# Spreading the late parts of 1/den through a copy inside DRAM, in a fused linear-attention and top-8 MLP kernel

## The chip, the cores and the metric

The kernel runs on one core of a Trainium2 chip. TensorE (PE) multiplies matrices, VectorE (DVE), ScalarE (ACT) and GpSimd (POOL) work on vectors, SyncE (SP) issues transfers. ScalarE and GpSimd can issue transfers too; what an engine issues goes out in the order of its own instructions, and an instruction that waits holds all behind it. All transfers run on the core's 16 DMA engines. The metric is the device time of one execution in microseconds (us), lower is better.

## The reference

One sequence of S = 2048 rows of D = 640. With 32 heads of 20 columns each:

```python
xn = layernorm(x)                                  # no gain, no bias
q, k, v = split(xn @ wqkv)                         # 32 heads of 20
pq, pk = phi(q), phi(k)                            # phi(t) = t + 1 if t > 0 else exp(t)
kv = einsum("hsd,hse->hde", pk, v);  z = pk.sum(s)
o = (pq @ kv) / (pq . z + 1e-6)                    # den: one number per row and head
A = o @ wo
idx = the 8 rows with the largest r = xn @ w_r
y = ((silu(xn[idx] @ w_gate) * (xn[idx] @ w_up)) @ w_down) * sigmoid(r[idx])
out = x + A + xn + scatter(y at idx)
```

Inputs and output are bf16.

## The kernel before

The rows are 16 tiles of 128 (`T`), the columns 5 chunks of 128 (`KC`). Instructions are issued in the order in which the program lists them; nothing reorders them within an engine.

The first 55 us or so load x, normalise it, and form k and part of q. The products over k are gathered into `G`, then into one matrix `Ms` that holds kv and wo together (`m_unit`, five units), so that the last stage is one product: tile t of the output is `pqT` (phi(q), transposed: columns of q on the partitions, rows of the sequence along the free axis) times `Ms`, plus x and xn. That stage is the loop `for t in range(T - 1)` with `o_mm(t)` (two halves of 320 columns, 10 matmuls) on TensorE and `o_out(t)` on VectorE, which adds `x_sb[:, t, :]` (by then x + xn) and hands the tile to a transfer. Its output buffer is one of four per parity of t, so tile t + 8 reuses that of tile t.

Before `o_mm(t)` the columns of `pqT` of that tile must be divided by den, which has one number per head and row while `pqT` has 20 partitions per head. The kernel spreads 1/den over the partitions through DRAM. `den_mm` forms den in PSUM, with the heads on 32 partitions and four groups of rows beside each other; `den_act` makes 1/den by Ln and Exp. For rows 0 to 1023 this is done once (`rden_out`, `rden_in`, ScalarE's queue out and SP's back). Rows 1024 to 1535 are the third quarter, `rden2`; rows 1536 to 2047 the fourth, `rden3`. Each of these leaves in four parts of 128 rows by `rden_out_b`: a part reads a 32 x 128 block and writes each of its rows 20 times into `rdb`, 640 rows of 256 bytes. `rden_in_b` brings 640 x 512 numbers back into `spare`, and `rden_mul_b(t)` on VectorE multiplies tile t of `pqT` by them, two tiles ahead of its use: after `o_out(6)` comes the multiply for tile 8, after `o_out(10)` that for tile 12.

The eight chosen rows go through the small MLP meanwhile: `gate_up`, then `down` (48 small matmuls after `o_mm(0)`), and ScalarE's four steps into `y8`. Tiles 11 to 15 of x + xn lie in DRAM as well (`s_dram`, written by `load_s`); GpSimd adds `y8` there, and `x_sb[:, 11:16]` is read back from it, so tiles from 11 on wait for that reload. For the tiles before, GpSimd adds `y8` to the output in DRAM, after `o_out(10)`.

[...]

The four parts of `rden2` are on SP, those of `rden3` on ScalarE and SP by turns. ScalarE issues the outputs of tiles 0 to 3 and the odd ones, and the reload of `x_sb`; SP those of 4, 6, ..., 14.

Of the kernel before, what the change touches and what calls it, by code (L numbers as in the profile page):

```python
# [8 lines left out]
P = 128  # L9
S = 2048  # L10
D = 640
H = 32
DH = D // H
F = 1536
T = S // P
KC = D // P
FC = F // P
# [9 lines left out]
TS = 11  # L27
NS = TS * P

BF16 = mybir.dt.bfloat16  # L30
# [8 lines left out]
def kernel(  # L39
# [12 lines left out]
    nc = tc.nc  # L52
    V, A, G, PE = nc.vector, nc.scalar, nc.gpsimd, nc.tensor
# [12 lines left out]
    def sb(name, shape, dtype=BF16):  # L66
        return sm.tile(shape, dtype, tag=name, name=name)

    ps = psum.tile([P, 8, 512], F32, tag="ps", name="ps")
    rd = tc.dram_tile([4, D, 256], BF16, name="rd")  # L70
    rdb = [tc.dram_tile([D, 512], BF16, name=f"rd{tb}") for tb in (2, 3)]
    s_dram = tc.dram_tile([S - NS, D], BF16, name="s_dram")

    x_sb = big.tile([P, T, D], BF16, tag="x_sb", name="x_sb")
# [9 lines left out]
    wu = big.tile([P, KC, F], BF16, tag="wu", name="wu")  # L84
# [3 lines left out]
    SP = nc.sync  # L88
# [20 lines left out]
    def kcw(w, src, lo, hi):  # L109
        SP.dma_start(w[:, lo:hi, :], src.rearrange("(kc p) n -> p kc n", p=P)[:, lo:hi, :])  # L110
# [7 lines left out]
    def load_wo():  # L118
        half = NB // 2
        for i in range(2):  # L120
            src = bass.AP(
                tensor=A_wo.tensor, offset=A_wo.offset + i * (D // 2) * D,
                ap=[[D, EB], [3 * DH * D, half], [1, D]],
            )
            SP.dma_start(wo[0:EB, i * half : (i + 1) * half, :], src)
# [4 lines left out]
    def load_wd(lo, hi):  # L130
        SP.dma_start(wd[:, lo:hi, :], B_w_down.rearrange("(fc p) n -> p fc n", p=P)[:, lo:hi, :])
# [139 lines left out]
    def q_mm(u, bank=7):  # L271
        tb, m = u // KC, u % KC
        for kc in range(KC):
            PE.matmul(  # L274
                ps[:, bank, :], lhsT=wq[:, kc, m * P : (m + 1) * P],
                rhs=xnT[:, kc, tb * 512 : (tb + 1) * 512],
                start=(kc == 0), stop=(kc == KC - 1),
            )

    def q_act(u, bank=7):  # L280
        e = evq.tile([P, 512], BF16, tag="eq", name=f"eq{u}")
        r = evq.tile([P, 512], BF16, tag="rq", name=f"rq{u}")
        A.activation(e[:], ps[:, bank, :], AF.Exp)  # L283
        A.activation(r[:], ps[:, bank, :], AF.Relu)  # L284
        kev["q", u] = e, r

    def q_phi(u):
        tb, m = u // KC, u % KC
        e, r = kev.pop(("q", u))
        V.scalar_tensor_tensor(  # L290
            out=pqT[:, m, tb * 512 : (tb + 1) * 512], in0=e[:], scalar=1.0, in1=r[:],
            op0=ALU.min, op1=ALU.add,
        )

    def q_ev(u, bank=7):
        q_act(u, bank)
        q_phi(u)
# [208 lines left out]

    load_cols(wv, 0, KC, 2 * D)
    load_wo()
    kcw(wu, B_w_up, 2, 3)
    kcw(wu, B_w_up, 3, KC)  # L510
    for i in range(0, FC, 4):
        load_wd(i, i + 4)
    PE.transpose(psb[0:T, 1, 0:P], r_all[:], ident[:])
    g1(T - 4)
    r_row = sb("r_row", [T, P], F32)
# [49 lines left out]
    def den_mm(o, w, bank):  # L565
        for kc in range(KC):
            for j in range(4):
                PE.matmul(
                    ps[32 * j : 32 * j + 32, bank, 0:w], lhsT=zm[:, kc, :],
                    rhs=pqT[:, kc, o + j * w : o + (j + 1) * w],  # L570
                    start=(kc == 0), stop=(kc == KC - 1), tile_position=(0, 32 * j),
                )

    def den_act(o, w, bank):
        ld = sm.tile([P, w], F32, tag="ld", name=f"ld{o}")
        rden = sb(f"rden{o}", [P, w])
        A.activation(ld[:], ps[:, bank, 0:w], AF.Ln, bias=cst["eps6"][:])
        A.activation(rden[:], ld[:], AF.Exp, scale=-1.0)
        return rden
# [11 lines left out]
            rd[j : j + 2, :, :].rearrange("j (m p) t -> p (j m) t", p=P),  # L591
        )

    def rden_out_b(eng, i, rden, j):
        eng.dma_start(  # L595
            rdb[i][:, j * P : (j + 1) * P].rearrange("(h i) t -> h i t", i=DH),
            rden[32 * j : 32 * j + 32, :].unsqueeze(1).to_broadcast([32, DH, P]),
        )

    def rden_in_b(i):  # L600
        SP.dma_start(sprb[i], rdb[i][:, :].rearrange("(m p) t -> p m t", p=P))

    def rden_mul(j):
        sl = pqT[:, :, j * 256 : (j + 1) * 256]
        V.tensor_tensor(out=sl, in0=sl, in1=spr[:, j * KC : (j + 1) * KC, :], op=ALU.mult)

    def rden_mul_b(t):
        sl = pqT[:, :, t * P : (t + 1) * P]
        V.tensor_tensor(  # L609
            out=sl, in0=sl, in1=sprb[t // 12][:, :, t % 4 * P : (t % 4 + 1) * P], op=ALU.mult  # L610
        )
# [18 lines left out]
    def m_unit(m, b0, eng):  # L630
        for h in range(2):
            for i in range(2):
                b = 2 * m + i
                PE.matmul(  # L634
                    ps[HB * i : HB * (i + 1), b0 + h, 0:HW], lhsT=kvz[0:EB, b * HB : (b + 1) * HB],
                    rhs=wo[0:EB, b, h * HW : (h + 1) * HW], start=True, stop=True,
                    tile_position=(0, HB * i),
                )
        dst = Ms[:, m, :].rearrange("p (b f) -> p b f", b=2)
        eng(dst, ps[:, b0 : b0 + 2, 0:HW])  # L640
# [80 lines left out]
                        start=(kc == 0), stop=(kc == KC - 1), tile_position=(0, 32 * j),  # L721
                    )

    def down():
        for fc in range(FC):
            for i in range(4):
                PE.matmul(
                    ps[32 * i : 32 * i + 32, 5 + 2 * (i % 2), 0:QW], lhsT=hT[:, 32 * fc : 32 * fc + 32],
                    rhs=wd[:, fc, i * QW : (i + 1) * QW],
                    start=(fc == 0), stop=(fc == FC - 1), tile_position=(0, 32 * i),  # L730
                    skip_group_check=True,
                )
# [29 lines left out]
    for u, b in ((13, 4), (14, 5), (15, 0), (16, 3)):  # L762
        q_mm(u, b)
        q_ev(u, b)
    m_unit(4, 6, V.tensor_copy)
    den_mm(1024, P, 4)
    rden2 = den_act(1024, P, 4)
    for j in range(4):
        rden_out_b(SP, 0, rden2, j)
    for u, b in ((17, 5), (18, 2), (19, 4)):  # L770
        q_mm(u, b)
        q_act(u, b)
        if u < 19:
            rden_mul(u - 17)
        q_phi(u)
    rden_in_b(0)

    def o_mm(t):
        b0 = 2 * (t % 2)
        for b in range(2):  # L780
            for kc in range(KC):
                PE.matmul(  # L782
                    ps[:, b0 + b, 0:HW], lhsT=pqT[:, kc, t * P : (t + 1) * P],
                    rhs=Ms[:, kc, b * HW : (b + 1) * HW],
                    start=(kc == 0), stop=(kc == KC - 1),
                )

    def o_out(t):
        b0 = 2 * (t % 2)
        o_t = evk.tile([P, 2, HW], BF16, tag=("ek", "rk")[t % 2], name=f"o{t}")  # L790
        V.tensor_tensor(  # L791
            out=o_t[:], in0=ps[:, b0 : b0 + 2, 0:HW],
            in1=x_sb[:, t, :].rearrange("p (b f) -> p b f", b=2), op=ALU.add,
        )
        eng = nc.sync if t % 2 == 0 and t > 2 else nc.scalar
        eng.dma_start(out_v[:, t, :], o_t[:].rearrange("p b f -> p (b f)"))

    def o_last(t):
# [24 lines left out]
    for t in range(T - 1):  # L823
        o_mm(t)
        if t == 0:
            down()
            den_mm(1536, P, 6)
            rden3 = den_act(1536, P, 6)
            for j in range(4):
                rden_out_b((A, SP)[j % 2], 1, rden3, j)  # L830
            rden_in_b(1)
            for i in range(4):
                A.activation(  # L833
                    y8[:, i * QW : (i + 1) * QW], ps[32 * i : 32 * i + C, 5 + 2 * (i % 2), 0:QW],
                    AF.Identity, scale=gate[32 * i : 32 * i + C, 2:3],
                )
            G.indirect_dma_start(  # L837
                s_dram[:, :], bass.IndirectOffsetOnAxis(ap=idx_i[0:C, 1:2], axis=0), y8[:], None,
                bounds_check=S - NS - 1, oob_is_err=False, compute_op=ALU.add,
            )  # L840
        if t == 5:
            A.dma_start(x_sb[:, TS:T, :], s_dram[:, :].rearrange("(t p) d -> p t d", p=P))
        o_out(t)
        if t < 2:
            rden_mul(t + 2)
        if 6 <= t < 14:
            rden_mul_b(t + 2)
        if t == TS - 1:
            G.indirect_dma_start(
                out[0, 0:NS, :], bass.IndirectOffsetOnAxis(ap=idx_i[0:C, 0:1], axis=0), y8[:], None,  # L850
                bounds_check=NS - 1, oob_is_err=False, compute_op=ALU.add,
            )
# [29 lines left out]
```

## Time and profile before

| | |
|---|---|
| timed runs, us | 113.39, 114.22, 117.89 (median 114.22) |
| the profiled execution, us | 112.75 |
| its span, from first to last instruction, us | 111.0 |
| granted TensorE clock | 1.00 |
| bytes moved by DMA | 23.65 MB, 213 GB/s in the mean |
| packets under 512 bytes | 14194 of 31655 |

The profile follows one execution, whose own time is 112.75 us; its span leaves out 1.75 us around it. "Busy" counts the time in which an engine had an instruction at work. SPq and ACTq are the transfers' issue instructions on SP and ScalarE. A DMA's "landing" is the time from its issue to its completion, so it holds the time in which it stood behind others. Line numbers (L595) are those of the kernel before.

### The profile page before, as it was taken

What the parts mean: (1) busy time and instruction counts of PE and PEld (TensorE: products, weight loads), DVE (VectorE), ACT (ScalarE), POOL (GpSimd) and SP (SyncE); (2) the same over time, 40 slices, a digit from 0 to 9 for tenths busy, and PEclk for the clock granted to TensorE, in tenths of its full rate; (3) what the DMA queues carried; (4) which work ended last, traced back from release to release, by engine and by line L of the source; (5) the groups of instructions that cost most, each with busy time, mean ns of one, the idle gap of its engine ahead of it and who ended that gap; (6) DMA issues with size and microseconds to landing.
All of it is one profiled execution on the core that took longest, in us unless ns stands there. A gap on an engine that the chain in (4) does not pass through costs nothing.

```text
span 111.0 us, 2501 instructions
## 1 busy us (share of the span) xinstructions
PE 104.3 (94%) x897; PEld 61.8 (56%) x906; DVE 81.2 (73%) x186; ACT 58.9 (53%) x155; POOL 39.2 (35%) x86
## 2 busy tenths in 40 slices
PE   5899999999999999999999999999999999994990
PEld 2256645555555555564447788534457776662660
DVE  1798997789999996544349745696799766884780
ACT  1449996797877666555058352788894400000000
POOL 6903563211344448899993420000000050000040
PEclk9999999999999999999999999999999999999999
DMA  3999435792679998999999949369868199999243
GB/s 81 324 328 297 152 68 101 197 240 59 183 189 203 210 177 206 224 220 302 235 388 365 304 110 287 98 173 302 292 91 151 51 344 254 242 359 386 89 124 118
DMA packets 31655, 23.65 MB, mean 213 GB/s; under 512 B 14194, under 2 KB 30362, under 8 KB 31642
## 3 DMA queue, kind: packets, MB, share of 16 engines
q1 hardware_dynamic: 25168, 18.97, 64.3%
q10 hardware_dynamic: 6410, 4.51, 13.2%
q8 instruction: 7, 0.11, 0.5%
q14 instruction: 6, 0.05, 0.2%
q0 software_dynamic: 64, 0.01, 0.2%
HBM read 15.44 MB, written 6.08 MB: 194 GB/s over the span
## 4 chain that ended last, share of the span: by engine, by line
PE 73%; DMA 14%; ACT 3%; issue 3%; DVE 2%; ACTq 2%; SPq 0%
PE ps L274 19%; PE ps L237 19%; PE ps L266 16%; PE ps L782 5%; DMA spare<-rd 5%; DMA out_dram<-o 4%; PE ps L502 4%; DMA rd<-rden 3%; DMA x_sb<-in_A_x_dram 2%; PE ps L617 2%; PE ps L634 2%; PE ps L717 2%; PE ps L215 1%; PE ps L808 1%; ACTq L595 1%
## 5 line engine op out<-in xcount | busy, mean ns | idle before, releaser
L237 PE MATMUL ps<-wk,xnT 128*128 128x320 bf16 (+1 forms) x160 | 25.0, 300 | 0.1
L274 PE MATMUL ps<-xnT,wq 128*128 128x512 bf16 x93 | 22.9, 379 | 0.6 <-issue 0.3
L782 PE MATMUL ps<-late,pqT 128*128 128x320 bf16 x150 | 21.6, 299 | 1.4 <-DVE pqT L609 1.4
L237 PEld LDWEIGHTS <-xnT 128*128 128x128 bf16 x160 | 15.1, 98 | 8.7 <-ACT xnT L221 0.9
L266 PE MATMUL ps<-pk,xn 128*128 128x512 bf16 x78 | 19.5, 379 | 0.1
L251 ACT ACTIVATE ek<-ps 128x320 bf16<-128x320 f32 x32 | 14.8, 463 | 8.1 <-PE ps L237 8.1
L782 PEld LDWEIGHTS <-pqT 128*128 128x128 bf16 x150 | 14.1, 98 | 8.7 <-DVE pqT L609 3.1
L283 ACT ACTIVATE eq<-ps 128x512 bf16<-128x512 f32 x20 | 11.9, 597 | 9.0 <-PE ps L274 9.0
L175 DVE BATCH_NORM_STATS2 stats<-x_sb 128x6 f32<-128x320 bf16 x32 | 14.8, 474 | 2.3 <-DMA x_sb<-in_A_x_dram 2.3
L290 DVE SCALAR_TENSOR_TENSOR pqT<-eq,rq 128x512 bf16<-128x512 bf16 x20 | 13.7, 685 | 3.7 <-ACT rq L284 3.7
L259 DVE SCALAR_TENSOR_TENSOR pk<-ek,rk 128x640 bf16<-128x640 bf16 x16 | 13.0, 813 | 4.2 <-ACT rk L252 4.2
L791 DVE TENSOR_TENSOR o<-ps,x_sb 128x640 bf16<-128x640 f32 x15 | 12.3, 823 | 4.7 <-PE ps L782 3.5
L274 PEld LDWEIGHTS <-wq 128*128 128x128 bf16 x100 | 9.3, 98 | 10.7 <-issue 0.7
L252 ACT ACTIVATE rk<-ps 128x320 bf16<-128x320 f32 x32 | 14.8, 463 | 0.0
L207 POOL TENSOR_SCALAR x_sb<-x_sb,rs,nm 128x640 bf16<-128x640 bf16 x13 | 13.8, 1068 | 0.6
L266 PEld LDWEIGHTS <-xn 128*128 128x128 bf16 x80 | 7.7, 98 | 8.1
L284 ACT ACTIVATE rq<-ps 128x512 bf16<-128x512 f32 x20 | 11.9, 593 | 0.0
L186 POOL TENSOR_SCALAR t<-mv 128x1 bf16<-128x1 f32 x12 | 3.8, 316 | 21.7 <-DVE mv L177 21.4
L818 ACT CAST o<-ps 128x160 bf16<-128x160 f32 x1 | 0.3, 292 | 19.1 <-PE ps L808 19.1
L187 POOL TENSOR_TENSOR rs<-t,mhalf 128x1 f32<-128x1 bf16 x12 | 10.0, 834 | 1.0
L837 POOL DMA_INDIRECT s_dram<-y,idx_i x1 | 1.6, 1594 | 23.2 <-ACT y L833 23.2
L196 DVE TENSOR_SCALAR xn<-x_sb,mv,rs 128x640 bf16<-128x640 bf16 x16 | 7.2, 450 | 3.3 <-POOL rs L187 2.8
(123 smaller groups left out, 98.6 us busy)
## 6 DMA issues: line engine op xcount, KB each, us to landing
spare<-rd SPq DMA_DIRECT2D x4, 640.0 KB, 5.4
wg<-in_B_w_gate_dram SPq DMA_DIRECT2D x5, 384.0 KB, 3.4
wd<-in_B_w_down_dram SPq DMA_DIRECT2D x3, 640.0 KB, 13.5
out_dram<-o ACTq DMA_DIRECT2D x9, 160.0 KB, 4.0
rd<-rden ACTq DMA_DIRECT2D x1, 1280.0 KB
wu<-in_B_w_up_dram SPq DMA_DIRECT2D x3, 384.0 KB, 3.5
wo<-in_A_wo_dram SPq DMA_DIRECT2D x2, 500.0 KB, 7.7
x_sb<-in_A_x_dram SPq DMA_DIRECT2D x3, 320.0 KB, 5.8
```

The source lines that it names most:

```text
L175: V.bn_stats(out=stats[:, t, b, :], in_=x_sb[:, t, b * HW : (b + 1) * HW])
L207: G.tensor_scalar(out=x_sb[:, t, :], in0=x_sb[:, t, :], scalar1=rs1[:, sl], scalar2=nm[:, sl], op0=ALU.mult, op1=ALU.add,)
L237: PE.matmul(ps[:, b0 + b, 0:n], lhsT=xnT[:, kc, t * P : (t + 1) * P], rhs=wk[:, kc, b * HW : b * HW + n], start=(kc == 0), stop=(kc == KC ...
L251: A.activation(e[:, b, :], ps[:, b0 + b, 0:HW], AF.Exp)
L252: A.activation(r[:, b, :], ps[:, b0 + b, 0:HW], AF.Relu)
L259: V.scalar_tensor_tensor(out=pk[:, t, :].rearrange("p (b f) -> p b f", b=2), in0=e[:], scalar=1.0, in1=r[:], op0=ALU.min, op1=ALU.add,)
L266: PE.matmul(ps[:, 2 + c, :], lhsT=xn[:, t, c * P : (c + 1) * P], rhs=pk[:, t, 0:512], start=(t == 0), stop=(t == T - 1),)
L274: PE.matmul(ps[:, bank, :], lhsT=wq[:, kc, m * P : (m + 1) * P], rhs=xnT[:, kc, tb * 512 : (tb + 1) * 512], start=(kc == 0), stop=(kc == K ...
L283: A.activation(e[:], ps[:, bank, :], AF.Exp)
L290: V.scalar_tensor_tensor(out=pqT[:, m, tb * 512 : (tb + 1) * 512], in0=e[:], scalar=1.0, in1=r[:], op0=ALU.min, op1=ALU.add,)
L782: PE.matmul(ps[:, b0 + b, 0:HW], lhsT=pqT[:, kc, t * P : (t + 1) * P], rhs=Ms[:, kc, b * HW : (b + 1) * HW], start=(kc == 0), stop=(kc == ...
L791: V.tensor_tensor(out=o_t[:], in0=ps[:, b0 : b0 + 2, 0:HW], in1=x_sb[:, t, :].rearrange("p (b f) -> p b f", b=2), op=ALU.add,)
```

## The change

- `rden_out_b` now writes each part of a late quarter once per head, 32 rows of 256 bytes, into a small DRAM tensor `rdh` (32 x 512). A new `rden_copy` reads each of its rows 20 times and writes `rdb` with 640 rows of 1,024 bytes, DRAM to DRAM, on SP.
- The four parts of `rden3` are all on ScalarE; `rden_copy(1)` is on SP, behind `rden_in_b(0)`, and `rden_in_b(1)` comes after tile 0's output.
- `den_mm(1536)` stands in the middle of `down`; `den_mm(1024)` ahead of `m_unit(4)`.
- SP issues the outputs of tiles 0, 2, 3, 6, 8, 9, 10, 12, 14, ScalarE those of 1, 4, 5, 7, 11, 13. The reload of `x_sb` moves from ScalarE to SP, behind the outputs of tiles 2 and 3 there.
- The late loads of `wu` (1 + 2 chunks) become one, those of `wd` two instead of three.

Rows 0 to 1023 of 1/den go as before. The engines' instructions are otherwise the same, in the same order. On SP the order from the third quarter on is: four parts of `rden2`, copy of the third quarter, its reload, copy of the fourth, output of tile 0, the fourth's reload, outputs of tiles 2 and 3, reload of `x_sb`, outputs of 6, 8, 9, 10, 12, 14, first half of 15.

```diff
+    rdh = [tc.dram_tile([H, 512], BF16, name=f"rdh{tb}") for tb in (2, 3)]
...
-    kcw(wu, B_w_up, 2, 3)
-    kcw(wu, B_w_up, 3, KC)
-    for i in range(0, FC, 4):
-        load_wd(i, i + 4)
+    kcw(wu, B_w_up, 2, KC)
+    for i in range(0, FC, 6):
+        load_wd(i, i + 6)
...
-    def rden_out_b(eng, i, rden, j):
-        eng.dma_start(
-            rdb[i][:, j * P : (j + 1) * P].rearrange("(h i) t -> h i t", i=DH),
-            rden[32 * j : 32 * j + 32, :].unsqueeze(1).to_broadcast([32, DH, P]),
+    def rden_out_b(eng, i, rden):
+        for j in range(4):
+            eng.dma_start(rdh[i][:, j * P : (j + 1) * P], rden[32 * j : 32 * j + 32, :])
+
+    def rden_copy(i):
+        SP.dma_start(
+            rdb[i][:, :].rearrange("(h i) t -> h i t", i=DH),
+            rdh[i][:, :].unsqueeze(1).to_broadcast([H, DH, 512]),
         )
...
-    def down():
-        for fc in range(FC):
+    def down(lo, hi):
+        for fc in range(lo, hi):
...
+    den_mm(1024, P, 4)
     m_unit(4, 6, V.tensor_copy)
-    den_mm(1024, P, 4)
     rden2 = den_act(1024, P, 4)
-    for j in range(4):
-        rden_out_b(SP, 0, rden2, j)
+    rden_out_b(SP, 0, rden2)
+    rden_copy(0)
     for u, b in ((17, 5), (18, 2), (19, 4)):
...
-    rden_in_b(0)
...
-        eng = nc.sync if t % 2 == 0 and t > 2 else nc.scalar
+        eng = nc.sync if t in (0, 2, 3, 9) or t % 2 == 0 and t > 4 else nc.scalar
...
         if t == 0:
-            down()
+            down(0, FC // 2)
             den_mm(1536, P, 6)
+            down(FC // 2, FC)
             rden3 = den_act(1536, P, 6)
-            for j in range(4):
-                rden_out_b((A, SP)[j % 2], 1, rden3, j)
-            rden_in_b(1)
+            rden_out_b(A, 1, rden3)
+            rden_in_b(0)
+            rden_copy(1)
...
+        if t == 2:
+            rden_in_b(1)
         if t == 5:
-            A.dma_start(x_sb[:, TS:T, :], s_dram[:, :].rearrange("(t p) d -> p t d", p=P))
+            SP.dma_start(x_sb[:, TS:T, :], s_dram[:, :].rearrange("(t p) d -> p t d", p=P))
```

## The prediction

> **What bounds the kernel now.** I read the page's busy table, then the chain of waits, the waits by engine and queue, the timeline of the last 35 us, and the DMA answers.
>
> ```profile
> span 111.0 us, 2501 instructions
> ...
> PE 104.3 (94%) x897; PEld 61.8 (56%) x906; DVE 81.2 (73%) x186; ACT 58.9 (53%) x155; POOL 39.2 (35%) x86
> ```
>
> TensorE is busy for 104.3 of 111.0 us. A change that leaves its work alone, as this one does, can win only the idle time. The chain shows where the one long gap near the end comes from (start, length, what):
>
> ```profile
> 93.08 3.19 DMA rd<-rden
> ...
> 96.33 5.34 DMA spare<-rd
> ...
> 101.69 0.50 DVE pqT L609
> ```
>
> The last quarter of 1/den is written to DRAM, read back as `spare`, multiplied into `pqT` for tile 12, and only then TensorE goes on. The waits (total, times, longest) give its price and what delayed it:
>
> ```profile
> PE ps L782 <- DVE pqT L609: 1.4, 1, 1.4
> ```
>
> ```profile
> SPq L595 <- DMA rd<-rden: 5.6, 1, 5.6
> ```
>
> SP stood 5.6 us before it could issue its two parts of that quarter (at 92.15 below), held by a part that ScalarE had issued at 86; the change takes this wait away, since no part is on SP any more. The hole itself is 1.43 us (the timeline below has it to two digits), and the ceiling of the gain in this execution is 1.43 of 112.75 us, 1.3%. The timeline rows used for the rest (start, length, engine, line):
>
> ```profile
> 79.50 0.37 ACT L577 ACTIVATE ld<-ps,eps 128x128 f32<-128x128 f32 x1
> ...
> 79.91 0.31 ACT L578 ACTIVATE rden<-ld 128x128 bf16<-128x128 f32 x1
> 80.24 3.16 SPq L595 DMA_DIRECT2D rd<-rden  x4
> ...
> 83.92 1.01 PE L727 MATMUL ps<-wd,late 128*32 128x160 bf16 x48
> ...
> 85.14 15.67 PE L782 MATMUL ps<-late,pqT 128*128 128x320 bf16 x110
> ...
> 85.71 0.31 ACT L578 ACTIVATE rden<-ld 128x128 bf16<-128x128 f32 x1
> 86.05 1.40 ACTq L595 DMA_DIRECT2D rd<-rden  x2
> 86.12 0.37 SPq L601 DMA_DIRECT2D spare<-rd  x1
> ...
> 89.42 1.59 POOL L837 DMA_INDIRECT s_dram<-y,idx_i  x1 [23.25 <-ACT y L833]
> ...
> 92.15 1.48 SPq L595 DMA_DIRECT2D rd<-rden  x2
> ...
> 93.63 0.39 ACTq L842 DMA_DIRECT2D x_sb<-s_dram  x1
> ...
> 94.31 0.48 DVE L609 TENSOR_TENSOR pqT<-pqT,spare 128x640 bf16<-128x640 bf16 x1
> ...
> 95.09 0.82 DVE L791 TENSOR_TENSOR o<-ps,x_sb 128x640 bf16<-128x640 f32 x1 [0.29 <-PE ps L782]
> ...
> 99.39 0.82 DVE L791 TENSOR_TENSOR o<-ps,x_sb 128x640 bf16<-128x640 f32 x1 [0.17 <-issue]
> ...
> 102.10 0.82 DVE L791 TENSOR_TENSOR o<-ps,x_sb 128x640 bf16<-128x640 f32 x1
> ...
> 102.24 4.44 PE L782 MATMUL ps<-late,pqT 128*128 128x320 bf16 x30 [1.43 <-DVE pqT L609]
> ...
> 105.42 1.35 POOL L849 DMA_INDIRECT out_dram<-y,idx_i  x1 [14.40 <-DMA out_dram<-o]
> ```
>
> Without the hole TensorE would end tile 11 at 85.14 + 15.67 = 100.81 and start tile 12 there. Transfers and their time from issue to landing, then half-microsecond stretches of the whole core (last three columns: clock, DMA share, GB/s):
>
> ```profile
> spare<-rd SPq DMA_DIRECT2D x4, 640.0 KB, 5.4
> ...
> rd<-rden SPq DMA_DIRECT2D x6, 160.0 KB, 3.4
> ...
> x_sb<-s_dram ACTq DMA_DIRECT2D x1, 800.0 KB, 5.4
> ...
> out_dram<-o ACTq DMA_DIRECT2D x1, 80.0 KB, 1.6
> ...
> s_dram<-y,idx_i POOLq DMA_INDIRECT x1, 4.1
> ```
>
> ```profile
> 64.00:64.50 0.50, 0.50 (x7) 0.28 (x5) 0.50 (x2) 0.33 (x1) 0.09 (x1) 1.00 0.06 23
> 68.00:68.50 0.50, 0.50 (x17) 0.50 (x14) 0.19 (x1) 0.00 (x0) 0.00 (x0) 1.00 1.06 294
> 80.50:81.00 0.50, 0.50 (x4) 0.24 (x3) 0.50 (x2) 0.49 (x1) 0.00 (x0) 1.00 0.00 0
> 81.50:82.00 0.50, 0.50 (x4) 0.20 (x2) 0.50 (x2) 0.50 (x2) 0.00 (x0) 1.00 0.78 119
> 82.00:82.50 0.50, 0.50 (x4) 0.23 (x3) 0.50 (x2) 0.50 (x2) 0.00 (x0) 1.00 1.00 154
> 85.50:86.00 0.50, 0.50 (x6) 0.35 (x5) 0.44 (x1) 0.47 (x2) 0.00 (x0) 1.00 0.29 54
> ...
> 100.00:100.50 0.50, 0.50 (x5) 0.36 (x4) 0.21 (x1) 0.00 (x0) 0.00 (x0) 1.00 1.09 389
> ```
>
> They price a transfer in three parts. The broadcast issued at 80.24 begins to move at about 81.6 (0.78 of the slice from 81.50): a start of 1.35 us. It stops at about 85.65 (0.29 of the slice from 85.50) and the queue that waits for it goes on at 86.12: a finish of 0.45. Between them the data goes at 389 GB/s in the reload, 294 in the first broadcast (512-byte rows) and 154 in the late ones (256-byte rows). 640 KB then take 1.7, 2.2 and 4.3 us; a tile written out (160 KB) 0.42; 800 KB reloaded 2.1.
>
> **The change, step by step.** *First hop.* 1/den of the third quarter is ready at 79.91 + 0.31 = 80.22, as before: `den_mm` moves ahead of one unit of M, but ScalarE comes to it straight from q's evictions, with no idle time, at 79.50. Four issues replace four. Each costs between 0.37 (a reload's) and 0.79 (3.16 / 4); with 32 rows in place of 640 I take 0.4. The fourth starts at 81.4. It carries 8 KB; its landing lies between the 1.6 of the small write and the 3.4 of the old parts, and I take 1.6, the nearer in size: 83.0.
>
> [...]
>
> *Copy inside DRAM.* No row shows DRAM to DRAM. Its 640 KB in rows of 1,024 bytes should take no less than 1.7 us and, I take it, no more than the 4.3 of the 256-byte rows; as both sides use DRAM I take the middle, 3.0. Issue at 83.0, landing after 1.35 + 3.0 + 0.45 = 4.8, at 87.8.
>
> [...]
>
> *Third quarter's reload* is issued at 87.8 in place of 86.12 and takes 1.35 + 1.7 + 0.45 = 3.5 alone, 5.4 in the median: 91.3 to 93.2. It is first used at 94.31. The 1.7 us lost are hidden, with 1.1 to 3.0 to spare.
>
> *Fourth quarter.* `den_mm` stands after half of `down`, 0.5 us earlier (half of 1.01): 1/den at 85.71 + 0.31 - 0.5 = 85.5. ScalarE issues four parts (1.6 against 1.40 for two), the last at 86.7, landed at 88.3. What is queued behind them on ScalarE is `y8` and the outputs of tiles 1, 4, 5, 7; `y8` feeds the scatter, which so stays at about 89.4 and lands 4.1 later, 93.5. The copy is queued on SP behind the third quarter's reload (issue over at 88.2) and starts at 88.3. Its data come after that reload's (to 90.85) and one output (0.42): 91.3 to 94.3, landed at 94.75.
>
> *Fourth quarter's reload* is then issued at 94.75 in place of 96.33, with no 800 KB ahead of it: data 96.1 to 97.8, landed 98.25 in place of 101.67. VectorE wants it after tile 10's output, at 99.39 + 0.82 = 100.2. That hole closes.
>
> *What is late next.* SP's order puts the outputs of tiles 2 and 3 and the 800 KB reload of `x_sb` behind that transfer. Tile 10's output reuses the buffer of tile 2; its write ends at 98.25 + 0.42 = 98.7, before 99.39. Tile 3's ends at 99.1, tile 7's (ready at 95.09 + 0.82) shares the time for 0.4 more. The reload, 2.1 us, begins at 99.05, ends at 101.15 and lands at 101.6. Before, it was issued at 93.63 and in by 99.0. Tile 11's output needs it at 100.8, and behind it on VectorE stands the multiply for tile 13: output 0.82 + multiply 0.48 + 0.06 to TensorE, so tile 13 starts at 101.6 + 1.36 = 102.96. Before it starts at 102.24 + 4.44 / 3 = 103.72. The gain is 0.76, half the hole.
>
> *At nothing:* the joined loads of `wu` and `wd` move the same bytes, and DMA traffic is down to a share of 0.06 by 64.0, while `down` reads `wd` at 83.92; if that cover were gone, TensorE would wait for the overlap in full. ScalarE's free queue costs nothing either way, and GpSimd's last add (105.42) waits for outputs up to tile 10, written no later than before.
>
> **Sum.** 112.75 - 0.76 = 112.0 for the profiled execution. The three timed runs have a median of 114.22, 1.47 above it, so by the median 114.22 - 0.76 = 113.5.
>
> Each microsecond on one copy delays the x_sb reload by one, and both copies count: from 1.7 to 4.3 us a copy the reload lands between 99.0 and 104.2, and the change lies between -1.43 (the hole is all there is) and +1.84. Issue and first landing at their other ends (0.79, 3.4) add some 3 us more; I do not think both hold for 8 KB.
>
> **The rivals.**
> *The hole goes entirely.* If a copy takes 2.4 us or less, the reload lands by 100.9 and 1.43 are won: 111.3 on the profiled execution, 112.8 by the median. The three runs lie 0.64 to 5.1 us above the profiled one, and the last exposed DMA chain is the natural place for that; if their surplus is a longer hole, it goes as well and the median comes to 111.3 (-2.6%). [...] Against it: one trace can't say where other runs lose time.
>
> *Slower: the x_sb reload is the new bound.* Place: tile 11's output, fed by the reload that now stands last in SP's queue behind three DRAM hops in series. It decides when the reload lands after 102.36 (103.72 - 1.36). At the 256-byte price of a copy, 4.3 us, it lands at 104.2, and the time is 114.22 + 1.84 = 116.1; with the first landings at 3.4 as well, 1.8 more, 117.9. For it: the old late part also looked short and took 10 us from 86.05 to 96.27. Against: fewer and longer rows.
>
> *No change in effect:* the wait is merely renamed, the reload landing near 102.4; 114.2.
>
> **How the numbers follow.** Over 2% (2.3 us), about what a measurement of this kernel can tell from no change, is more than the hole in this trace, so faster needs the runs' surplus: 0.30. Slower by 2% needs the reload at 104.7, a copy of 4.6 us or a slow first hop: 0.23. Within 2%: the forecast (gain 0 to 1.5) 0.32, no change and a little slower 0.15; together 0.47. The range takes in the full hole with the surplus, 111.0, and the 256-byte copy, 116.5; the likeliest case alone spans 112.5 to 114.2.
>
> **What would show it.** Right: no wait of TensorE before tile 12; `spare<-rd` of the fourth quarter issued near 94.8; tile 11's output waiting for `x_sb<-s_dram` by some 0.8 us; copies landing near 4.8. Wrong: a multiply at 94.3 that waits for the third quarter (the first hops cost more than 1.1 us above mine); a copy far from 3.0 us of data; a wait for an output's buffer at tile 10; or TensorE as full as before with the time unmoved.

## The result, and the profile after

The changed kernel takes 118.47 us (median of 6 runs, 117.33 to 119.79), the kernel before on the same chip 113.81 (6 runs, 113.26 to 117.89): a ratio of 1.0415, 95% interval 1.034 to 1.049, slower. Some executions of the kernel before and of its variants, the long ends of such ranges, run at a lower mean clock (0.971 to 0.985 in ten of the kernel before's 23 on one chip, 0.997 and more in the others); the ratios compare executions without them, and a timeline of such a long one has its time beside it and shows where a wait lies, not what it costs. The profiled execution takes 118.92 us, 6.2 more than that of before.

The changed kernel's page: span, busy time of the engines, the granted clock in 40 slices, and the DMA packets.

```profile
span 117.2 us, 2497 instructions
...
PE 105.7 (90%) x897; PEld 62.3 (53%) x906; DVE 81.2 (69%) x186; ACT 58.9 (50%) x155; POOL 39.3 (34%) x86
...
PEclk9999999999999999999999999999999999999599
...
DMA packets 28072, 23.72 MB, mean 202 GB/s; under 512 B 9331, under 2 KB 26779, under 8 KB 28059
```

The small packets went as meant (9331 in place of 14194). TensorE's busy time grew by 1.4 us though it does the same matmuls, and one slice near the end has the clock at half. The waits (engine and line, what they waited for, total, times, longest; the last row is one of SP's queue):

```profile
PE ps L786 <- DVE pqT L614: 5.4, 2, 3.5
...
DVE o L795 <- DMA x_sb<-s_dram: 3.8, 1, 3.8
...
SPq L600 <- DMA rdh<-rden: 4.5, 3, 3.5
```

One hole of 1.43 us has become two, 5.4 us together. SP's wait of 5.6 us, which the prediction meant to take away, has become one of 3.5: the fourth quarter's copy stands on SP until the last part from ScalarE has landed. The timeline (start, length, engine, line) shows the hops and the two holes, at tile 12 and at tile 13:

```profile
80.84 1.73 SPq L597 DMA_DIRECT2D rdh<-rden  x4
...
83.67 0.64 SPq L600 DMA_DIRECT2D rd<-rdh  x1
...
86.23 2.27 ACTq L597 DMA_DIRECT2D rdh<-rden  x4
...
87.94 0.38 SPq L606 DMA_DIRECT2D spare<-rd  x1
...
91.92 0.54 SPq L600 DMA_DIRECT2D rd<-rdh  x1
...
97.55 0.36 SPq L606 DMA_DIRECT2D spare<-rd  x1
...
99.04 0.46 SPq L849 DMA_DIRECT2D x_sb<-s_dram  x1
...
102.76 0.49 DVE L614 TENSOR_TENSOR pqT<-pqT,spare 128x640 bf16<-128x640 bf16 x1 [1.96 <-DMA spare<-rd]
...
103.31 1.53 PE L786 MATMUL ps<-late,pqT 128*128 128x320 bf16 x10 [1.91 <-DVE pqT L614]
107.06 0.82 DVE L795 TENSOR_TENSOR o<-ps,x_sb 128x640 bf16<-128x640 f32 x1 [3.80 <-DMA x_sb<-s_dram]
...
108.34 4.50 PE L786 MATMUL ps<-late,pqT 128*128 128x320 bf16 x20 [3.50 <-DVE pqT L614]
```

The first row's 80.84 stands against 80.24 before. In a variant below with the same instructions up to there it is 80.19, so 0.6 us of the 6.2 belong to this execution and not to the hops. The rest: tile 12 waits 0.5 longer (1.91 for 1.43), tile 13 waits 3.50, and the 20 matmuls of tiles 13 and 14 take 4.50 us where 20 of the 30 took 2.96 before (4.44 x 2 / 3), 1.5 more. 0.6 + 0.5 + 3.5 + 1.5 = 6.1 of 6.2. Transfers (KB each, median us from issue to landing), and stretches of the core (last three columns: clock, DMA share, GB/s):

```profile
spare<-rd SPq DMA_DIRECT2D x4, 640.0 KB, 4.8
...
rd<-rdh SPq DMA_DIRECT2D x2, 640.0 KB, 4.9
...
x_sb<-s_dram SPq DMA_DIRECT2D x1, 800.0 KB, 7.8
...
rdh<-rden SPq DMA_DIRECT2D x4, 8.0 KB, 1.4
rdh<-rden ACTq DMA_DIRECT2D x4, 8.0 KB, 3.1
```

```profile
85.00:87.50 2.50, 2.50 (x65) 1.89 (x54) 1.66 (x4) 0.68 (x2) 0.00 (x0) 1.00 0.82 271
93.00:97.50 4.50, 4.50 (x32) 2.81 (x31) 3.70 (x6) 0.00 (x0) 0.00 (x0) 1.00 0.85 250
97.50:100.00 2.50, 2.50 (x19) 1.50 (x17) 2.04 (x5) 0.00 (x0) 0.00 (x0) 1.00 0.53 108
100.00:106.50 6.50, 2.93 (x20) 1.68 (x18) 1.29 (x2) 0.00 (x0) 0.00 (x0) 1.00 1.00 358
108.50:111.50 3.00, 3.00 (x12) 1.66 (x11) 1.19 (x3) 0.00 (x0) 1.35 (x1) 0.50 0.35 112
```

The first row is the third quarter's copy, nearly alone: 2.5 us x 271 GB/s = 678 KB (thousands of bytes, as in the products below), and 640 x 1.024 = 655 are its own. The second is the fourth's: 1,125 KB, which leaves 470 for three outputs of 164 beside it. The fourth row is one solid block of 6.5 us and 2,327 KB: the fourth quarter's reload (655), the reload of `x_sb` (819), and 853 left, five outputs. The block can't begin before the last copy has landed, at 97.55, and in the 2.5 us between that landing and the block the engines do little (the row ahead of it: a share of 0.53, 108 GB/s). The last row is the clock behind the long wait.

The chain of waits (start, length, what) puts another name on the long hole:

```profile
100.95 6.32 DMA out_dram<-o
...
107.80 0.49 DVE pqT L614
...
108.34 4.50 PE ps L786 x20
```

It names an output that landed at 107.27, where the waits name the reload, in by 107.06. Both are the end of the same block, so the name in one view does not decide which transfer is to blame; the run below with the kernel after's reload in two pieces does, since tile 11's output comes earlier with it.

### The profile page after: what moved, and what is told of

It reads as the page before. It is cut to its first block, busy times and chain, and to the rows that moved or that the text cites. A ratio compares the mean times of both kernels' runs of the same rounds, so it can differ in the third digit from the quotient of the medians.

```text
span 117.2 us, 2497 instructions
## 1 busy us (share of the span) xinstructions
PE 105.7 (90%) x897; PEld 62.3 (53%) x906; DVE 81.2 (69%) x186; ACT 58.9 (50%) x155; POOL 39.3 (34%) x86
## 2 busy tenths in 40 slices
DMA packets 28072, 23.72 MB, mean 202 GB/s; under 512 B 9331, under 2 KB 26779, under 8 KB 28059
## 4 chain that ended last, share of the span: by engine, by line
PE 81%; DMA 10%; ACT 2%; issue 2%; DVE 1%; SPq 1%; DVEq 0%
PE ps L275 18%; PE ps L238 18%; PE ps L786 17%; PE ps L267 15%; DMA out_dram<-o 5%; DMA wk<-in_A_wqkv_dram 5%; PE ps L503 4%; PE ps L622 2%; PE ps L639 2%; PE ps L722 1%; PE ps L812 1%; PE ps L568 1%; SPq L96 1%; PE ps L651 1%; PE ps L732 1%
## 5 line engine op out<-in xcount | busy, mean ns | idle before, releaser
L786 PE MATMUL ps<-late,pqT 128*128 128x320 bf16 x150 | 23.2, 314 | 5.4 <-DVE pqT L614 5.4
L786 PEld LDWEIGHTS <-pqT 128*128 128x128 bf16 x150 | 14.8, 102 | 13.7 <-DVE pqT L614 7.1
```

Of the source, the lines that this page charges most:

```text
L786: PE.matmul(ps[:, b0 + b, 0:HW], lhsT=pqT[:, kc, t * P : (t + 1) * P], rhs=Ms[:, kc, b * HW : (b + 1) * HW], start=(kc == 0), stop=(kc == ...
```

## Experiments

**The place of the reload, or the hops?** The kernel after differs from before in where things are queued and in how 1/den is spread. Three runs take these apart. First, the reload of `x_sb` back on ScalarE, all else as after:

```diff
-            SP.dma_start(x_sb[:, TS:T, :], s_dram[:, :].rearrange("(t p) d -> p t d", p=P))
+            A.dma_start(x_sb[:, TS:T, :], s_dram[:, :].rearrange("(t p) d -> p t d", p=P))
```

> The changed kernel with one line undone: the reload of x_sb is on ScalarE's queue again, as before the change. Theory A (the reload's place is the cost: last on SP, it lands at 106.9 and makes the 3.5 us wait of tile 13, and the clock drop behind that wait): tile 13 waits less than 0.5 us, the reload lands by 101, the wait of tile 12 grows from 1.9 to about 3 because the reload again goes ahead of the fourth quarter's, and the time is 115 to 116.5 us. Theory B (the three hops through DRAM are the cost wherever the reload stands): 118 us or more, the time that tile 13 loses reappears at tile 12.

116.14 us (113.39, 114.67, 117.62 and 118.38), ratio 1.0056 (0.997 to 1.014), that of the first two. In the timeline, of 118.38 us, the reload leaves at 92.95, and the fourth quarter pays:

```profile
98.51 0.36 SPq L606 DMA_DIRECT2D spare<-rd  x1
...
105.68 6.49 PE L786 MATMUL ps<-late,pqT 128*128 128x320 bf16 x30 [4.94 <-DVE pqT L614]
```

In this execution the wait has moved from tile 13 to tile 12: whichever reload is second lands late. In the two shorter ones most of the loss is gone, and no trace shows how their waits lie. So the reload's place is part of the cost, and this run does not settle how large a part.

Second, after's order and queues with the old spread (256-byte rows written 20 times, no copy):

```diff
-            eng.dma_start(rdh[i][:, j * P : (j + 1) * P], rden[32 * j : 32 * j + 32, :])
+            eng.dma_start(
+                rdb[i][:, j * P : (j + 1) * P].rearrange("(h i) t -> h i t", i=DH),
+                rden[32 * j : 32 * j + 32, :].unsqueeze(1).to_broadcast([32, DH, P]),
+            )
```

> The changed kernel with the old spreading: each part goes out 20 times in rows of 256 bytes, no small tensor and no copy; order and queues are those of the change (third quarter's parts on SP, fourth's on ScalarE, reload of x_sb on SP behind the last read). Theory A (place of the reload): still slow, 116.5 to 119 us, with tile 13 waiting for the reload by 2 us or more. Theory B (the hops): 113 to 115 us, as the hops are gone.

113.19 us (112.98 to 113.74, 4 runs), ratio 0.999 (0.995 to 1.003). Its timeline, and one stretch of it:

```profile
93.32 0.36 SPq L605 DMA_DIRECT2D spare<-rd  x1
...
95.13 0.39 SPq L848 DMA_DIRECT2D x_sb<-s_dram  x1
...
103.54 2.89 PE L785 MATMUL ps<-late,pqT 128*128 128x320 bf16 x20 [1.48 <-DVE pqT L613]
```

```profile
96.00:102.50 6.50, 6.06 (x42) 3.58 (x40) 4.08 (x8) 0.00 (x0) 0.00 (x0) 1.00 1.04 376
```

All of the loss is gone with the hops. The solid block is as long (6.5 us) but begins at 96.0 in place of 100.0, since the fourth's reload is issued 4.2 us earlier (93.32 for 97.55; 0.7 of it is that the first part's row stands at 80.11 here, the rest is the hops). The new queues do close the hole at tile 12, and open one of 1.48 at tile 13: for the time they are worth nothing.

The same kernel with the reload on ScalarE (the edit of the first run) asks whether the two edits add:

> The version with the change's order and queues but the old spreading, and with the x_sb reload on ScalarE's queue. In the old-spreading version tile 13 waited 1.5 us for a reload issued at 95.1 and landed 6.9 later. Theory: on ScalarE the reload is issued at about the same time but lands by 101, tile 13's wait falls under 0.5 us and the time to 112.0 to 112.8 us. Rival: it goes beside the fourth quarter's reload, which then lands 1 to 2 us later; the wait moves to tile 12 and the time stays at 113.0 to 114.0.

113.26 us (112.61 to 115.47, 12 runs), ratio 0.9977 (0.994 to 1.002); no difference that can be told. The reload waits until the scatter into `s_dram`, which it reads, has landed (91.61 + 4.9 = 96.5; it is issued at 96.57), and tile 13 waits 1.75 us. The scatter itself is late here: `y8` stands on ScalarE behind the four old parts, which take 4.2 us to issue, and it starts 2.2 us later than before (89.42). So this run says little of the queue.

**Which hop?** The copy of the fourth quarter stands on SP behind the third's reload. Here it stands ahead of it:

```diff
-            rden_in_b(0)
             rden_copy(1)
+            rden_in_b(0)
```

> The changed kernel with two lines swapped: on SP the fourth quarter's copy is issued ahead of the third quarter's reload. Theory C (the last small part of the fourth quarter stands behind the third quarter's reload on the DMA engines, which is why it landed 3 us later than its size says): the copy is issued at about 89.5 instead of 91.9, the fourth quarter's reload lands 2 to 3 us earlier, by 100.5, tile 12 waits under 0.5 us, the x_sb reload lands near 104, and the time is 114.5 to 116.5 us; the third quarter's reload lands some 1 to 3 us later and may make tile 8 wait up to 1 us. Rival (the small part is slow in itself): the copy is issued at 91.5 or later and the time is 118 us or more.

115.16 us (113.88 to 116.64, 4 runs), ratio 1.0119 (1.004 to 1.019). The timeline, of 116.64 us:

```profile
90.11 0.53 SPq L600 DMA_DIRECT2D rd<-rdh  x1
...
95.11 0.36 SPq L606 DMA_DIRECT2D spare<-rd  x1
...
98.69 11.74 PE L786 MATMUL ps<-late,pqT 128*128 128x320 bf16 x70 [3.61 <-DVE pqT L614]
```

The fourth's first part is issued at 85.74 (86.23 in after), and the copy 4.4 us behind it in place of 5.7; the fourth's reload leaves 2.4 earlier than in after; but the third's reload, now beside the copy, lands at 98.1, 7.5 us after its issue, and tile 8 waits 3.61 us, where up to 1 was expected. The time is the expected one; of the mechanism the first half holds.

Then the hops for one quarter only (HOP is 0 for the third, 1 for the fourth), the other spread as before:

> The changed kernel with the small tensor and the copy for the third quarter alone; the fourth quarter goes out 20 times in rows of 256 bytes, on ScalarE, without a copy. Theory D (the fourth quarter's hops are the cost, the third's are hidden): 113 to 114.5 us. Rival E (the third quarter's hops hold up SP's queue and with it all that follows): 116 us or more.

> The changed kernel with the small tensor and the copy for the fourth quarter alone; the third goes out 20 times in rows of 256 bytes, on SP, without a copy. Theory D: 116 to 119 us, the fourth quarter's reload issued at 96 us or later. Rival E: 113 to 114.5 us.

```diff
     def rden_out_b(eng, i, rden):
         for j in range(4):
+            if i == HOP:
                 eng.dma_start(rdh[i][:, j * P : (j + 1) * P], rden[32 * j : 32 * j + 32, :])
+            else:
+                eng.dma_start(
+                    rdb[i][:, j * P : (j + 1) * P].rearrange("(h i) t -> h i t", i=DH),
+                    rden[32 * j : 32 * j + 32, :].unsqueeze(1).to_broadcast([32, DH, P]),
+                )
     def rden_copy(i):
+        if i == HOP:
```

Third only: 114.26 us (113.14 to 116.22), ratio 1.0018 (0.996 to 1.008). Fourth only: 116.31 (114.20, 114.69, 117.93 and 118.12), ratio 1.011 (1.005 to 1.017), that of the first two; 4 runs each. The timeline of the second, of 118.12 us:

```profile
89.81 0.54 SPq L607 DMA_DIRECT2D rd<-rdh  x1
...
95.97 0.36 SPq L613 DMA_DIRECT2D spare<-rd  x1
...
107.42 4.54 PE L793 MATMUL ps<-late,pqT 128*128 128x320 bf16 x20 [4.25 <-DVE pqT L621]
```

By the ratios the fourth quarter's hops alone cost some 1% and the third's nothing that can be told, though the intervals overlap. Together that is a third of 4.15%: the rest comes only with both, and no run takes it further apart. In this execution the copy left 2.1 us earlier than in after, but the reload only 1.6, since the copy took 6.1 to land where after's took 5.6; and the `x_sb` reload behind it took 8.5.

**The small parts.** In after the fourth of ScalarE's parts is issued last in a row of 2.27 us and lands at 91.9 at the latest, when the copy starts. Here two of the four go on SP, ahead of the third's reload:

```diff
-            rden_out_b(A, 1, rden3)
+            for j in range(4):
+                (A, SP)[j % 2].dma_start(
+                    rdh[1][:, j * P : (j + 1) * P], rden3[32 * j : 32 * j + 32, :]
+                )
```

> The changed kernel with the fourth quarter's four small parts shared by ScalarE and SP by turns, two each, SP's ahead of the third quarter's reload. Theory C (the last small part is late because it is issued fourth in a row on ScalarE and meets the third quarter's 640 KB reload): all parts land by 88.5, the fourth quarter's copy is issued by 89.0 instead of 91.9, its reload by 95.5 instead of 97.5, and the time is 115 to 117 us. Rival (the copy itself and what moves beside it set the chain): the copy goes out early but lands 7 us later or more, the reload is issued at 96 or later, 117.5 us or more.

117.5 us (114.38, and three from 117.36 to 117.86), against 114.0 for the kernel before beside it; too few runs for a ratio. The timeline, of 117.63 us:

```profile
89.30 0.54 SPq L600 DMA_DIRECT2D rd<-rdh  x1
...
95.63 0.36 SPq L606 DMA_DIRECT2D spare<-rd  x1
...
107.01 4.30 PE L786 MATMUL ps<-late,pqT 128*128 128x320 bf16 x20 [3.88 <-DVE pqT L614]
```

The parts, issued at 85.62, land in time for a copy 3.7 us later, where after's takes 5.7; the copy then takes 6.3 us beside the third's reload, the `x_sb` reload 8.3, and tile 13 waits as long as ever. What is won at the first hop is given back to sharing here; the execution of 114.38 has no trace.

**Queue order and completion.** Is the reload of `x_sb` late because five outputs follow it on its own queue? Outputs of tiles 6, 8, 9 and 10 on ScalarE:

```diff
-        eng = nc.sync if t in (0, 2, 3, 9) or t % 2 == 0 and t > 4 else nc.scalar
+        eng = nc.sync if t in (0, 2, 3) or t % 2 == 0 and t > 10 else nc.scalar
```

> The changed kernel with the outputs of tiles 6, 8, 9 and 10 on ScalarE's queue instead of SP's, so that nothing is issued behind the x_sb reload on its own queue until tile 12. Theory H (those outputs overtake the reload because they share its queue; that is why it took 7.8 us to land): the reload lands within 6 us of its issue, tile 13 waits 2 us less than in the changed kernel, 116 to 117 us. Rival (all transfers share the 16 DMA engines whichever queue issued them, and the reload is late because it was issued late and 640 KB of outputs pass at the same time): it still takes 7 us or more from issue to landing, 117.5 us or more.

121.06 us (120.49 to 121.10, 4 runs), ratio 1.0647 (1.060 to 1.070), the slowest of all. Its timeline:

```profile
103.66 2.52 PE L786 MATMUL ps<-late,pqT 128*128 128x320 bf16 x10 [3.01 <-DVE pqT L614]
...
109.19 5.24 PE L786 MATMUL ps<-late,pqT 128*128 128x320 bf16 x19 [3.02 <-DVE pqT L614]
```

The reload lands after 8.3 us, no sooner than on a queue with the outputs (7.8), and the matmuls behind both holes are slow: the outputs on its queue are not what holds the reload.

**The clock.** Twelve extra matmuls on zeros between tiles 12 and 13; they feed nothing:

```diff
     for t in range(T - 1):
+        if t == 13:
+            warm(12, 4)
         o_mm(t)
```

> The changed kernel with 12 extra matmuls of zeros into an unused PSUM bank between tile 12 and tile 13, where TensorE waits 3.5 us; they feed nothing. Theory G (the wait itself costs 3.5 us, and the granted clock, which falls to half behind it, costs another 1.5 us): the clock stays at 1.0, the 20 matmuls of tiles 13 and 14 take 2.9 us instead of 4.5, and the time is 116.5 to 117.5 us. Rival (the slow matmuls come from something else, late weights or DMA contention): 20 matmuls at 4.2 us or more, 118 to 119 us.

116.4 us (115.59 to 117.48, 4 runs), ratio 1.0259 (1.020 to 1.032), against after's 1.0415. TensorE's timeline, of 117.48 us:

```profile
102.77 1.88 PE L786 MATMUL ps<-late,pqT 128*128 128x320 bf16 x10 [2.12 <-DVE pqT L614]
...
108.41 2.88 PE L786 MATMUL ps<-late,pqT 128*128 128x320 bf16 x20
```

Tile 13 starts as late as in after (108.41 for 108.34), the reload being no sooner, but its 20 matmuls take 2.88 us in place of 4.50. The clock did not stay at 1.00 in this execution: after tile 12's wait of 2.12 it was 0.78 from 102.7 to 104.7 and 0.50 from 104.7 to 107.0, mostly over the extra matmuls, which feed nothing. The other three executions have a mean clock of 1.000. So some 1.6 us of after's loss are the clock.

**The edits put at nothing.** Before, with the joined loads and the two moves of `den_mm` and nothing else:

```diff
-    kcw(wu, B_w_up, 2, 3)
-    kcw(wu, B_w_up, 3, KC)
-    for i in range(0, FC, 4):
-        load_wd(i, i + 4)
+    kcw(wu, B_w_up, 2, KC)
+    for i in range(0, FC, 6):
+        load_wd(i, i + 6)
...
+    den_mm(1024, P, 4)
     m_unit(4, 6, V.tensor_copy)
-    den_mm(1024, P, 4)
...
-            down()
+            down(0, FC // 2)
             den_mm(1536, P, 6)
+            down(FC // 2, FC)
```

> The kernel before with only the parts that the prediction put at nothing: the joined loads of wu and wd, the third quarter's den ahead of a unit of M, the fourth's in the middle of down. Theories A and B: 113.0 to 114.5 us, the same as before. [...]

116.09 us (115.13 to 116.81, 4 runs), ratio 1.0233 (1.017 to 1.030): not the "same" that was expected. The third's reload leaves at 88.61 in place of 86.12, tile 12 waits 2.20 us, and the 30 matmuls behind it take 5.92 us for 4.44, at a clock of 0.58 from 103 to 106 and 0.86 from 106 to 109:

```profile
103.03 5.92 PE L781 MATMUL ps<-late,pqT 128*128 128x320 bf16 x30 [2.20 <-DVE pqT L608]
```

The moves of `den_mm` without the loads:

> The kernel before with only the two moves of den (ahead of a unit of M; into the middle of down). [...] Rival (the joined loads made the kernel with all moves slow): 113 to 114 us.

114.54 us (114.11 to 116.16, 4 runs), ratio 1.0106 (1.006 to 1.015). The timeline:

```profile
88.73 0.36 SPq L601 DMA_DIRECT2D spare<-rd  x1
...
103.57 4.43 PE L782 MATMUL ps<-late,pqT 128*128 128x320 bf16 x30 [2.64 <-DVE pqT L609]
```

The third's reload is 2.6 us late with the loads as before. In the trace the fourth quarter's first part, issued on ScalarE at 85.8, lands 2.8 us later, at 88.6, and the reload goes out at 88.73; in the kernel before that part lands only at 91.5, and the reload, at 86.12, does not wait for it. That the reload waits for that part here is the reading that fits; the trace does not name what it waits for. So `den_mm`'s place costs 1% here; a hole of much the same length then cost more in the run with the loads, where the clock fell to 0.58, than in this one, where the 30 matmuls took 4.43 us and the mean clock was 0.996. What the loads alone cost was not tried.

**The spread of the kernel before** (112.5 to 119.2 over 23 runs): are its long executions a clock that falls behind the hole at tile 12? Five extra matmuls that feed nothing, ahead of tile 12 in the kernel before:

```diff
     for t in range(T - 1):
+        if t == 12:
+            warm(5, 4)
         o_mm(t)
```

> The kernel before with 5 extra matmuls of zeros into an unused PSUM bank ahead of tile 12, where TensorE waits 1.4 us; they feed nothing. Theory G (the 2 to 5 us by which some executions of the kernel before are longer are a granted clock at half speed behind a longer wait): no execution shows a mean clock under 0.99, and the highest time is under 114.5 us, at an unchanged median of 113.0 to 113.8. Rival (the long executions have another cause): some executions still above 115 us.

115.33 us (112.85 to 118.76, 12 runs), ratio 0.998 (0.994 to 1.002): six of the twelve are still at 116.65 and more. This fill does not cure them; their cause stays open.

**Less in the block.** If the last transfer is late because it is long, tile 11 and 12's part of it (320 of 800 KB) can go first. On the old spread with after's queues:

```diff
-            SP.dma_start(x_sb[:, TS:T, :], s_dram[:, :].rearrange("(t p) d -> p t d", p=P))
+            SP.dma_start(
+                x_sb[:, TS : TS + 2, :], s_dram[0 : 2 * P, :].rearrange("(t p) d -> p t d", p=P)
+            )
+            SP.dma_start(
+                x_sb[:, TS + 2 : T, :], s_dram[2 * P :, :].rearrange("(t p) d -> p t d", p=P)
+            )
```

> The version with the change's order and queues but the old spreading, and with the x_sb reload on SP in two transfers, tiles 11 and 12 (320 KB) first, then 13 to 15. Theory: tile 11's output gets its rows by 100 instead of 102.0, tile 13's wait of 1.5 us goes, and the time is 111.8 to 112.6 us. Rival: the first piece lands as late as the whole did, since outputs issued later pass it on the DMA engines: 113.0 to 113.8 us.

111.92 us (111.34 to 112.48, 6 runs), ratio 0.9851 (0.981 to 0.989): faster than both kernels. The timeline:

```profile
101.71 0.82 DVE L794 TENSOR_TENSOR o<-ps,x_sb 128x640 bf16<-128x640 f32 x1 [0.86 <-DMA x_sb<-s_dram]
...
102.99 2.89 PE L785 MATMUL ps<-late,pqT 128*128 128x320 bf16 x20 [0.55 <-DVE pqT L613]
```

Tile 11's output has its rows at 101.7, not by 100 as expected, and the hole at tile 13 goes from 1.48 to 0.55, not to nothing. The same split on the kernel after:

> The changed kernel with the x_sb reload in two transfers, tiles 11 and 12 (320 KB) first, nothing else. Theory A in part (tile 11 waits for 800 KB where it needs 160): the first piece lands 2 us earlier than the whole did, tile 13 waits 1 to 2 us instead of 3.5, 115.5 to 117 us. Rival (both pieces are late because the transfer ahead of them is): tile 13 still waits over 2.5 us, 117.5 us or more.

115.38 us (115.05 to 115.77, 4 runs), ratio 1.0168 (1.011 to 1.022), about 3 us better than after. In its timeline tile 11's output starts at 103.92, 2.5 us earlier than in after when the 0.6 us are taken off, and the matmuls behind both holes run at full speed:

```profile
102.62 1.53 PE L786 MATMUL ps<-late,pqT 128*128 128x320 bf16 x10 [1.81 <-DVE pqT L614]
...
105.20 2.89 PE L786 MATMUL ps<-late,pqT 128*128 128x320 bf16 x20 [1.05 <-DVE pqT L614]
```

And the best that the hops got, with the small parts on both queues as well:

> g1_parts_both and the x_sb reload in two transfers, tiles 11 and 12 first. If the two causes add up and nothing else is left: no wait of TensorE over 1 us in the last stage, clock 1.0, 112 to 113.5 us, no faster than the old-spreading version with the split reload (111.9). If the copy inside DRAM costs by itself: 114 us or more.

113.74 us (112.75 to 114.47, 12 runs), ratio 1.0032 (0.999 to 1.007). The time lies between the two that were expected, and tile 13 still waits 1.37 us. With every late step mended that the runs had found, the copy only draws level with the kernel before, and stays behind the same split without a copy (1.0032 against 0.9851).

## Why the prediction failed

The forecast was 113.5 and the kernel takes 118.47. The mechanism was among the rivals ("the x_sb reload is the new bound"), with its place right and its chance too small. Times of the profile are set back by the 0.6 us above.

- *First hop, third quarter*: right. Forecast 83.0, measured 83.67 - 0.6 = 83.1; 1.4 us for 8 KB.
- *Copy inside DRAM*: right for the third, slightly high. Landing 87.94 - 83.67 = 4.3 for 4.8, data 2.4 us for 3.0. The price that looked least known was not the error.
- *Third quarter's reload* hidden: right; the multiply for tile 8 starts at 94.90 - 0.6 = 94.3, as before.
- *Fourth quarter*, the first step that failed: "the last at 86.7, landed at 88.3". The copy behind it started at 91.3, 3.0 later: the issues took 2.27 us for 1.6, and a part landed in 3.1 us in the median, the last in 4.2, where 1.6 was taken. I had priced a small transfer alone, and these move beside the third's copy and reload: the last part lands in 4.2 us in after, in 2.9 with the copy ahead of that reload, and in 1.5 in the run with the fourth's hops only, where the engines were nearly idle (a mean share under 0.1 and 19 GB/s from 87.3 to 90.2). From the first part's issue to the copy's it is 5.7 us in after, 4.4 with the copy ahead of the reload, 3.7 with the parts shared between two queues (2.8 in the forecast). As the forecast had the copy stand in a queue for 1.65 us anyway, the reload behind it was issued 2.2 late (96.95 for 94.75), with a landing of 5.6 for the copy beside three outputs.
- *What is late next*, the second: "The reload, 2.1 us, begins at 99.05, ends at 101.15 and lands at 101.6". It was in at 107.06 - 0.6 = 106.5. I let transfers run one behind the other in queue order. In the trace they run together: the outputs issued behind the reload, from 99.63 on, move beside it and land within a microsecond of it. The block that ends with the reload was to take 96.1 to 101.15, three outputs in it, and took 99.4 to 105.9 with five, 3.3 us of late start and 1.4 of length. The rival's own bound (late after 102.36) then gives 106.5 - 102.36 = 4.1, near the two holes' 0.5 + 3.5.
- *Sum*: it has no term for the clock, 1.5 us here. 112.75 + 0.6 + 4.1 + 1.5 = 118.95, of 118.92.
- *At nothing*: the moves and the joined loads together are worth nothing with the old spread, as said; but `den_mm`'s moves alone are not free. The hole at tile 12 did not go entirely: the new queues close it, the hops open it again.
- *Signs*: of those named for being right only the copies came near (4.3 and 5.6 us for 4.8); tile 12 waits 1.91 us, and tile 11's output 3.80 for 0.8. Those named for being wrong did not come, except that the fourth's copy, beside three outputs, is slower than forecast: they looked at the third quarter and at tile 10, and the failure was in the fourth quarter and behind it.
- *Two smaller slips*: since both copies count, the first rival needs copies of 2.7 us, not 2.4 (101.6 - 2 x 0.33 = 100.9). And the surplus of 1.47 us is no sign of a longer hole: executions of the kernel before with a mean clock of 0.997 and more lie between 112.51 and 115.31 us on one chip.

The start of a reload was mis-sized as well, and the trace of before shows it. The 1.35 us came from a write to DRAM. The third quarter's reload there is issued at 86.12, and nothing much moves for 2.3 us (last three columns: clock, DMA share, GB/s):

```profile
87.50:88.00 0.50, 0.50 (x5) 0.35 (x4) 0.50 (x2) 0.49 (x2) 0.00 (x0) 1.00 0.00 0
...
88.50:89.00 0.50, 0.50 (x6) 0.35 (x5) 0.50 (x1) 0.47 (x2) 0.00 (x0) 1.00 0.91 322
```

In after the reloads begin to move 2.3 us (87.94 to about 90.25) and some 2.5 us (97.55 to about 100) after their issue, the copies 1.4. So of the 3.3 us of late start, 2.2 are the late issue and 1.1 this term.

The range's upper end was made from the price of a copy alone. What was uncertain was three hops in series, each priced alone, that run in company, and what a hole of 2 to 3.5 us does to the clock.

Open: why the fourth's copy lands in 5.6 to 6.3 us was read from the stretch (three outputs beside it, or the third's reload), and no run had it alone; how much of the loss is the reload's place and how much the hops, as undoing either takes most or all of it away in the executions that the ratios compare; and the long executions of the kernel before.

## What to carry to other kernels

A hop through DRAM is worth its landing in company, not its bytes (8 KB landed in 1.4 to 4.2 us here): fewer and longer packets saved a third of the small ones here and cost 4%, because each hop's landing stood in series ahead of the last block of transfers. When several transfers are needed near the end, ask when their joint block can start and what must be in first; sending the piece that the next tile needs ahead of the rest won 1.5%, with nothing else made faster. Where a hole of TensorE is moved, look at the clock behind it as well: it fell behind waits of 2.12, 2.20 and 3.50 us here, not behind 1.91, and not behind one of 2.64.

## What was not expected of the hardware

- The granted clock fell behind some waits and not behind others, and not in the order of their lengths. The 20 matmuls after a wait of 3.50 us ran at 0.50 for 3 us (108.5 to 111.5). After 2.12, in the run with the extra matmuls, it was 0.78 from 102.7 to 104.7, then 0.50 to 107.0, and the 30 matmuls after 2.20 took 5.92 us for 4.44, at 0.58 in the first 3 us. After 1.91 ten matmuls took 1.53 us, unhurt, and after 2.64 thirty took 4.43. Why 2.64 escaped, where 2.12 and 2.20 did not, no run here shows.
- Taking outputs off the reload's queue did not make it land sooner: its 800 KB landed in 5.4 us before, in 7.8 in after, where the fourth's reload and the outputs move with it on one queue, and in 8.3 with four of those outputs on the other queue.
- A copy from DRAM to DRAM in rows of 1,024 bytes moved at 271 GB/s nearly alone, close to the 294 of the first broadcast's writes.
